# Attention with routing: one last group of nine tiles, and VectorE's extra operations behind a tile's normalisation

## The chip, the cores and the metric

The kernel runs on one core of a Trainium2 chip. Its metric is the device time in microseconds of one execution; the median of three runs of the kernel before is 1285.98 us (1285.92 to 1286.72). The engines are named as the profile names them: PE is TensorE's matmuls and PEld its weight loads, DVE is VectorE, ACT is ScalarE, POOL is GpSimd, and SP issues most of the DMAs.

## The reference, cut to what matters

Three layers follow each other, with 8 batches of 576 tokens, so 4608 tokens of 512 numbers.

```python
# 1: attention, K and V averaged over 8 neighbours first (q, k, v: 8 x 8 heads x 576 x 64)
k_p = k.reshape(B, H, Sp, 8, D).mean(axis=3)
v_p = v.reshape(B, H, Sp, 8, D).mean(axis=3)
s = scale * q @ k_p^T;  s -= max(s);  a = exp(s);  a /= sum(a) + 1e-9
x = a @ v_p                                   # -> 4608 x 512
# 2: mixture of 8 experts
do = x @ w_skip > 0                           # tokens that are computed at all
e = argmax(x @ w_gate);  p = softmax(x @ w_gate)[e]
out = x;  out[do] = x + p * (relu(x @ w1[e]) @ w2[e])      # 512 -> 1024 -> 512
# 3: a dense layer
h = out @ w_in;  g = h * sigmoid(h);  y = g @ w_out        # 512 -> 2048 -> 512
```

## The kernel before, in words

Every operation of an engine is issued through a helper on line 115, so nearly all rows of the profile carry L115 and are told apart by the names of what they write and read. The helper keeps the order in which the code issues them: what stands first in the program for an engine runs first on it.

**Stage 1, attention** (until about 152 us). The 4608 tokens are 36 tiles of 128. Turn i of the loop issues, on PE, the scores `s` of tile i+3, the transposes `pt` of the exponentials of tile i+1, and `pv`, the product with V, of tile i. `pv` has a single PSUM buffer, so that `pv` of tile i+1 waits until DVE has read `pv` of tile i. On DVE the turn issues `mx` (the maxima of tile i+3's scores), some extra operations, and then `post` of tile i: `sm` (sum plus 1e-9), its reciprocal, `cc` (eight router scores and the skip score, per head), `x` (the normalised output, the last reader of `pv`) and `lg` (the router scores of the tile). ACT computes the exponentials `prb` and copies `pts`.

The extra operations are of these kinds. `kp` averages a part of K for a later batch (`pool_k`; the table `KEYS` says in which turns, and six turns have two). `w1l` prepares expert weights in three of the last turns and once more behind. `self.slow` hands out two small operations a turn (`SLOW = 2`). And there is the routing of a group of tiles, in `todo`: when a group's last `lg` is done, `step1` (8 operations, `rmx` to `sb`) finds the expert of each token and writes the one-hot `rohb`, in the next turn `count` lets PE count the tokens of each expert (`rps`, one matmul by `trib` and one by `onesb` for each tile of the group), and `step2` (9 operations, `tot` to `ix`) turns the counts into a place for each token. The numbers A1, A2 and A3 say how many operations of `step1`, of `step2` and of two other small sequences (`choose`, `early`) stand ahead of `post` in their turn; the rest of them stand behind it. For each tile of the group an indirect DMA on POOL then scatters the 128 token numbers to their places in `slots` in DRAM: one or two a turn in the loop, and all of those that are left at the end.

The tiles were grouped as 9, 9, 9, 6 and 3: the fourth group ends with tile 32, and its routing runs in the turns of tiles 33 and 34. The last group of three is routed at the handover.

**Handover** (about 152 to 190 us). The first unit of the experts' layer has its expert chosen and its tokens gathered early (`xn`). PE runs its first layer (`hp`, eight parts f), with `hl` and `hh` made by DVE and ACT. In between, the last group is routed: `step1`, `mm1(0, 1)`, `count`, `step2`, all its scatters. `read_table` on POOL then reads all of `slots` back as `table`, when the scatters have landed. `units` is a long row of tiny DVE operations that plans the other units. DVE's order behind that is: `hl` of part 6, a copy of two thirds of `xr` (`keep`, whose last third is on ACT), `w2l` of parts 0 to 3 (the low halves of the second layer's weights), the rest of `units`, `taken` (`sc` and `table`, which read what `read_table` has brought), the row numbers `gi`, `hl` of part 7, `w2l` of parts 4 to 7. PE's second layer `yp` needs `w2l` part by part. POOL gathers the next unit's tokens by `gi`.

**Stages 2 and 3.** A hardware loop (L1023) runs the other units, and from about 510 us on the dense layer keeps PE busy to the end.

Of the kernel before, what the change touches and what calls it, by code (L numbers as in the profile page):

```python
# [37 lines left out]
U = 3  # L38
# [4 lines left out]
KEYS = {2: (2, 3, 4, 4), 3: (6, 6, 7, 8), 4: (11, 12, 13, 13), 5: (15, 15, 16, 17), 6: (20, 20, 21, 22),  # L43
        7: (24, 24, 25, 26)}
# [8 lines left out]
OPS = [2, 2, 2, 0, 4, 4]  # L53
ORDER = list(range(NT // 512))[::-1]
SLOW = 2
A1, A2, A3 = 8, 5, 12

C_E, C_MV, C_LID, C_WT, C_THR, C_LE, C_UN, C_PK, C_TRI = 0, 2, 13, 49, 57, 153, 217, 241, 265
C_N = C_TRI + P
# [29 lines left out]


GROUP = {}
for _g, (_t0, _n) in enumerate([(0, 9), (9, 9), (18, 9), (27, 6), (33, 3)]):
    GROUP.update({_t0 + _j: (_g, _j, _n) for _j in range(_n)})


# [62 lines left out]
class Kern:  # L158
# [19 lines left out]
    def attention(self, xa, rs, extra):  # L178
        nc, tc, c = self.nc, self.tc, self.c
        self.todo = todo = []  # L180
        self.slow = iter(())
        with tc.tile_pool(name="as", bufs=1) as s1, \
# [31 lines left out]
            def pool_k(b, eng, halves=(0, 2), n=2):  # L214
                k = k_t[b]
                kp = st.get((b, "k"))
                if kp is None:
                    kp = st[b, "k"] = s2.tile([P, 4, G], F32, name=f"kp_{b}", tag="kp")
                if eng is nc.vector:
                    for a in halves:  # L220
                        eng.tensor_reduce(kp[:, a:a + n], k[:, a:a + n], AX.X, ALU.add)
                else:
                    eng.tensor_tensor(k[:, :, :, 0:4], k[:, :, :, 0:4], k[:, :, :, 4:8], ALU.add)
                    eng.tensor_tensor(k[:, :, :, 0:2], k[:, :, :, 0:2], k[:, :, :, 2:4], ALU.add)
                    eng.tensor_tensor(kp, k[:, :, :, 0], k[:, :, :, 1], ALU.add)
# [98 lines left out]
            def pv(t, pt):  # L324
                ps = pp.tile([P, 1024], F32, name=f"pv_{t}", tag="pv")
                ps = ps[:, 0:H * HW].rearrange("p (h e) -> p h e", e=HW)
                for i, j, h0, n, start, stop in PVS:
                    for b, o, r, m in parts(t):
                        ve = vex[b % NB]
                        nc.tensor.matmul(ps[r:r + m, h0:h0 + n, 0:VW], pt[:CP, i, r:r + m], ve[:CP, j:j + n],  # L330
                                         start=start, stop=stop, skip_group_check=True)
                st["pv"] = ps
# [56 lines left out]
            for i in range(-2, NTILE):  # L389
                if i == -2:  # L390
                    pool_v(0, ON0)
                n = 3 if i > DEEP else 2
                if i > 0 and i + n < NTILE:
                    pss = products(i + n)
                    pts[i + 1] = ptrans(i + 1, prs.pop(i + 1))
                    prs[i + n] = scores(i + n, pss)
                elif i != -1 and i <= DEEP:
                    prs[i + 2] = scores(i + 2)
                if len(self.to_place) > (3 if i < EARLY else 0) and i < NTILE - 1:
                    self.place(1, nc.scalar.last)  # L400
                extra(i, True)
                ready = todo.pop(0) if todo and i < NTILE - 1 else None
                if ready and ready[0]:
                    ready[0]()
                if i == -2:
                    values(0)
                    loadv(1)
                    loadq(1)
                if i == -1:
                    pss = products(1)  # L410
                    router1(0)
                if i == 0:
                    pv(0, pts.pop(0))
                if 0 <= i + 1 < NTILE and i + 1 not in pts:
                    pts[i + 1] = ptrans(i + 1, prs.pop(i + 1))
                if i == -1:
                    prs[1] = scores(1, pss)
                    router2(0)
                    pool_k(1, nc.vector, (0,))
                    pool_v(1, ON1)  # L420
                    values(1)
                if i > 0:
                    pv(i, pts.pop(i))
                a = ready[1]() if ready and ready[1] else iter(())
                b = post(i) if i >= 0 else iter(())
                for _ in range(ready[2] if ready else 0):
                    next(a, None)
                for _ in range(SLOW):
                    next(self.slow, None)
                for bb, tiles in KEYS.items():  # L430
                    for r, t in enumerate(tiles):
                        if i == t:
                            pool_k(bb, nc.vector, (r,), 1)
                for _ in b:
                    pass
                for _ in a:
                    pass
                for bb, tiles in KEYS.items():
                    if i == tiles[-1]:
                        keys(bb)  # L440
                if i == 0:
                    pool_k(1, nc.vector, (2,))
                    keys(1)
                for b in range(B):
                    if i + 4 == first[b] and 0 < b < B - 1:
                        loadq(b + 1)
                    if 0 <= i + 2 - first[b] < 2 and 0 < b < B - 1:
                        pool_v(b + 1, 0, ((0,), (1, 2))[i + 2 - first[b]])
                    if i + 2 == first[b]:
                        if b + 2 < B:  # L450
                            loadk(b + 2)
                            loadv(b + 2)
                    if i + 2 == first[b] + 3 + (b == 0) and b + 1 < B:
                        router1(b + 1)
                    if i + 2 == first[b] + 3 and 0 < b < B - 1:
                        values(b + 1)
                    if i + 2 == first[b] + 5 and b + 1 < B:
                        router2(b + 1)
                if i == DEEP:
                    prs[i + 3] = scores(i + 3)  # L460
                if i == EARLY + 7:
                    self.read_table(nc.sync)
                if i == 2:
                    nc.sync.dma_start(self.cb, self.con[:, P + C_TRI:])
                if i == 6:
                    self.consts()
                if i < NTILE - 1:
                    self.place(1, nc.vector.last)
                else:
                    self.place(len(self.to_place))  # L470
                extra(i)
# [373 lines left out]
    def moe(self, xa, up):  # L845
        nc, tc, c = self.nc, self.tc, self.c
        with tc.tile_pool(name="ms", bufs=1) as s1, \
             tc.tile_pool(name="mw", bufs=2) as s2, \
             tc.tile_pool(name="mp", bufs=2, space=PSUM) as pp:
            raw2, xn, xth, xtl, gi, si = self.raw2, self.xn, self.xth, self.xtl, self.gi, self.si  # L850
# [3 lines left out]
            xr = s1.tile([P, U, XW], F32, name="xr", tag="xr")  # L854
            y = self.x4[:, 0:U]

            def keep():
                nc.scalar.copy(xr[:, U - 1], xn[:, U - 1])
                nc.vector.tensor_copy(xr[:, 0:U - 1], xn[:, 0:U - 1])
# [89 lines left out]
            def low2(f):  # L949
                nc.vector.tensor_tensor(self.w2l[:, f], raw2[:, f], self.w2h[:, f].bitcast(F32), ALU.subtract)  # L950

            keep()
            for f in range(4):
                low2(f)
            while not next(units):
# [698 lines left out]
```

## Time and profile before

| | before |
|---|---|
| median of 3 runs | 1285.98 us |
| profiled execution | 1285.66 us |
| its span, first to last instruction | 1283.9 us |
| mean granted TensorE clock | 0.997 |
| PE busy | 1244.5 us, 97% of the span |
| DVE busy | 850.9 us, 66% |
| ACT busy | 576.4 us, 45% |
| POOL busy | 354.8 us, 28% |

The times in the rows are microseconds from the start of the span. A row of the timeline is one instruction or several alike: start, duration, engine, what it writes and reads, shape, count. In square brackets stands how long the engine was idle just before it, and what released it. A row of the windows gives, for each engine, the busy time in a stretch and how many instructions it holds, and then the granted clock of TensorE (1.00 is 2.4 GHz, 0.50 is 1.2 GHz), the mean busy share of the DMA engines and GB/s.

### The profile page before, as it was taken

What the parts mean: (1) busy time and instruction counts of PE and PEld (TensorE: products, weight loads), DVE (VectorE), ACT (ScalarE), POOL (GpSimd) and SP (SyncE); (2) the same over time, 40 slices, a digit from 0 to 9 for tenths busy, and PEclk for the clock granted to TensorE, in tenths of its full rate; (3) what the DMA queues carried; (4) which work ended last, traced back from release to release, by engine and by line L of the source; (5) the groups of instructions that cost most, each with busy time, mean ns of one, the idle gap of its engine ahead of it and who ended that gap; (6) DMA issues with size and microseconds to landing.
All of it is one profiled execution on the core that took longest, in us unless ns stands there. A gap on an engine that the chain in (4) does not pass through costs nothing.

```text
span 1283.9 us, 20146 instructions
## 1 busy us (share of the span) xinstructions
PE 1244.5 (97%) x6469; PEld 1058.2 (82%) x6470; DVE 850.9 (66%) x1559; ACT 576.4 (45%) x1224; POOL 354.8 (28%) x313
## 2 busy tenths in 40 slices
PE   6999899999999989999999999999999999999998
PEld 6988778998888978778888887888888888888887
DVE  5888876666776777889624245656775567846565
ACT  5877534455545554444433344433444233433321
POOL 5477432222222312223377312010201011110100
PEclk9999999999999999999999999999999999999999
DMA  9888536565765634349564225462555444462532
GB/s 372 316 299 287 194 105 236 176 202 173 241 220 187 198 113 144 140 159 305 201 246 145 85 91 174 146 213 93 178 183 186 163 141 139 148 225 94 181 118 88
DMA packets 94716, 234.45 MB, mean 183 GB/s; under 512 B 15093, under 2 KB 27509, under 8 KB 90928
## 3 DMA queue, kind: packets, MB, share of 16 engines
q1 hardware_dynamic: 87344, 216.47, 48.7%
q0 software_dynamic: 7008, 16.80, 4.0%
q8 instruction: 43, 0.70, 0.2%
q14 instruction: 33, 0.27, 0.1%
q10 hardware_dynamic: 288, 0.20, 0.0%
HBM read 183.24 MB, written 52.89 MB: 184 GB/s over the span
## 4 chain that ended last, share of the span: by engine, by line
PE 58%; DVE 2%; issue 1%; ACT 1%; POOL 0%; DMA 0%; ACTq 0%; DVEq 0%; POOLq 0%
PE yb L115 21%; PE ps L115 17%; PE fop L115 8%; PE fh L115 8%; PE hp L115 1%; PE yp L115 1%; DVE fr L115 1%; DVE ft L115 1%; PE fxp L115 1%; DVE fsg L115 0%; PE sx L115 0%; ACT fm L115 0%; DVE fgl L115 0%; ACT g L115 0%; DMA out<-fo 0%
## 5 line engine op out<-in xcount | busy, mean ns | idle before, releaser
L115 PE MATMUL yb<-wout,g 128*128 128x512 f32 x1152 | 268.5, 391 | 0.7 <-DMA wout<-wdo 0.5
L115 PEld LDWEIGHTS yb<-wout,g 128*128 128x128 f32 x1152 | 215.0, 188 | 45.6 <-DMA wout<-wdo 0.9
L115 POOL TENSOR_TENSOR tm<-tm,tm 128x512 f32<-128x512 f32 x24 | 32.2, 1340 | 411.7 <-ACT tm L115 411.7
L115 DVE TENSOR_TENSOR yacc<-yb,yacc 128x512 f32<-128x512 f32 x168 | 116.0, 691 | 38.7 <-PE yb L115 31.4
L115 ACT COPY tm<-ps 128x512 f32<-128x512 f32 x72 | 42.3, 588 | 146.4 <-PE ps L115 144.5
L115 ACT CAST g<-sg 128x512 fp32r<-128x512 f32 x96 | 59.6, 621 | 76.8 <-DVE sg L115 76.8
L115 DVE TENSOR_TENSOR fsg<-fh,fsg 128x512 f32<-128x512 f32 x48 | 33.0, 688 | 83.3 <-ACT fsg L115 80.8
L115 DVE TENSOR_TENSOR w2l<-raw,w2h 128x512 fp32r<-128x512 f32 x96 | 65.8, 690 | 29.0 <-ACT w2h L115 25.5
L115 ACT ACTIVATE hh<-hp 128x256 fp32r<-128x256 f32 (+1 forms) x96 | 39.4, 410 | 98.9 <-PE hp L115 89.2
L115 PE MATMUL fh<-w1l,fh 128*128 128x512 f32 x336 | 83.4, 390 | 0.0
L115 PE MATMUL yp<-w2h,hh 128*128 128x512 f32 x208 | 83.1, 400 | 0.0
L115 PE MATMUL yp<-w2l,hh 128*128 128x512 f32 x208 | 81.2, 391 | 1.9 <-DVE w2l L115 1.9
L115 DVE TENSOR_TENSOR tm<-ps,tm 128x512 f32<-128x512 f32 x24 | 16.6, 691 | 98.1 <-PE ps L115 98.1
L115 PE MATMUL yp<-w2h,hl 128*128 128x512 f32 x208 | 81.3, 391 | 0.0
L115 PE MATMUL hp<-xth,w1h 128*128 128x256 f32 (+2 forms) x384 | 72.5, 311 | 6.6 <-PEq L1650 3.3
L115 PE MATMUL hp<-xtl,w1h 128*128 128x256 f32 (+2 forms) x384 | 72.0, 308 | 3.1 <-DVE xtl L115 1.9
L115 PEld LDWEIGHTS fh<-w1l,fh 128*128 128x128 f32 x336 | 62.8, 188 | 12.9
L115 PE MATMUL hp<-xth,w1l 128*128 128x256 f32 (+2 forms) x384 | 71.2, 308 | 0.0
L115 ACT ACTIVATE prb<-s,mx 128x72 f32<-128x72 f32 x288 | 65.3, 355 | 11.0 <-DVE mx L115 11.0
L115 DVE TENSOR_TENSOR g<-sg,g 128x512 fp32r<-128x512 f32 x96 | 65.8, 686 | 5.1 <-ACT g L115 4.8
L115 PEld LDWEIGHTS hp<-xth,w1h 128*128 128x128 f32 x384 | 60.4, 192 | 9.4 <-issue 7.6
L115 PE MATMUL fop<-fh,fgh 128*128 128x512 f32 x168 | 66.4, 395 | 1.2 <-ACT fgh L115 1.2
(240 smaller groups left out, 2723.1 us busy)
## 6 DMA issues: line engine op xcount, KB each, us to landing
raw<-w SPq DMA_DIRECT2D x88, 512.0 KB, 4.4
wout<-wdo SPq DMA_DIRECT2D x48, 512.0 KB
win<-wdi SPq DMA_DIRECT2D x36, 512.0 KB
w1l<-wdi SPq DMA_DIRECT2D x36, 512.0 KB
xa<-x SPq DMA_DIRECT2D x36, 256.0 KB
fx<-xa SPq DMA_DIRECT2D x9, 1024.0 KB
v<-vR SPq DMA_DIRECT2D x7, 1280.0 KB
fr<-w_in SPq DMA_DIRECT2D x16, 512.0 KB
```

Of the source, the lines that this page charges most:

```text
L115: ins = f(*a, **k)
```

## The change: what it does

There are five edits. The numbers A1, A2, A3 become 5, 0, 5. The last two groups become one group of nine. `count` is issued behind `pv` of its turn. Of the extra operations only the first part of `kp` and the first A operations of the routing stand ahead of `post`; the second `kp`, the rest of the routing and then the two slow operations stand behind it. At the handover the copy to `xr` is three ACT copies instead of one on ACT and one on DVE.

```diff
-A1, A2, A3 = 8, 5, 12
+A1, A2, A3 = 5, 0, 5
...
-for _g, (_t0, _n) in enumerate([(0, 9), (9, 9), (18, 9), (27, 6), (33, 3)]):
+for _g, (_t0, _n) in enumerate([(0, 9), (9, 9), (18, 9), (27, 9)]):
...
                 ready = todo.pop(0) if todo and i < NTILE - 1 else None
-                if ready and ready[0]:
-                    ready[0]()
...
                 if i > 0:
                     pv(i, pts.pop(i))
+                if ready and ready[0]:
+                    ready[0]()
                 a = ready[1]() if ready and ready[1] else iter(())
                 b = post(i) if i >= 0 else iter(())
                 for _ in range(ready[2] if ready else 0):
                     next(a, None)
+                todays = [(bb, r) for bb, tiles in KEYS.items() for r, t in enumerate(tiles) if i == t]
+                for bb, r in todays[:1]:
+                    pool_k(bb, nc.vector, (r,), 1)
+                for _ in b:
+                    pass
+                for bb, r in todays[1:]:
+                    pool_k(bb, nc.vector, (r,), 1)
+                for _ in a:
+                    pass
                 for _ in range(SLOW):
                     next(self.slow, None)
-                for bb, tiles in KEYS.items():
-                    for r, t in enumerate(tiles):
-                        if i == t:
-                            pool_k(bb, nc.vector, (r,), 1)
-                for _ in b:
-                    pass
-                for _ in a:
-                    pass
...
-            keep()
+            for j in range(U):
+                nc.scalar.copy(xr[:, j], xn[:, j])
             for f in range(4):
                 low2(f)
```

On DVE, in the turn of tile 10, which has the second step of the first group's routing, the kernel before runs five operations of that step (`tot` to `pi`) ahead of the tile's `sm`:

```order
L115 TENSOR_REDUCE mx_790<-s_774 128x4
L115 TENSOR_REDUCE mx_790<-s_777 128x4
L115 TENSOR_TENSOR tot_76<-tot_75,rps_801 128x8
L115 TENSOR_TENSOR ra_819<-rps_801,tot_75 128x72
L115 TENSOR_TENSOR ra_819<-ra_819,rohb_759 128x72
L115 TENSOR_REDUCE ri_822<-ra_819 128x9
L115 TENSOR_SCALAR pi_824<-ri_822 128x9
L115 TENSOR_SCALAR sm_826<-pv_812 128x8
L115 RECIPROCAL sm_826<-sm_826 128x8
L115 TENSOR_TENSOR cc_827<-pv_812,sm_826 128x72
L115 TENSOR_TENSOR x_84<-pv_812,sm_826 128x512
L115 TENSOR_REDUCE lg_769<-cc_827 128x9
```

In the changed kernel the same place reads:

```order
L115 TENSOR_REDUCE mx_790<-s_774 128x4
L115 TENSOR_REDUCE mx_790<-s_777 128x4
L115 TENSOR_SCALAR sm_818<-pv_801 128x8
L115 RECIPROCAL sm_818<-sm_818 128x8
L115 TENSOR_TENSOR cc_819<-pv_801,sm_818 128x72
L115 TENSOR_TENSOR x_84<-pv_801,sm_818 128x512
L115 TENSOR_REDUCE lg_763<-cc_819 128x9
L115 TENSOR_TENSOR tot_76<-tot_75,rps_807 128x8
L115 TENSOR_TENSOR ra_827<-rps_807,tot_75 128x72
L115 TENSOR_TENSOR ra_827<-ra_827,rohb_768 128x72
L115 TENSOR_REDUCE ri_830<-ra_827 128x9
L115 TENSOR_SCALAR pi_832<-ri_830 128x9
```

The five operations have moved from ahead of `sm` to behind `lg`, where the other four of the step follow them, as before.

On PE, in the same turn, the kernel before runs the count (`rps`, by `trib` and then nine times by `onesb`) between the transposes and `pv`:

```order
L115 MATMUL pt_781<-ident,prb_117 120x128 x3
L115 MATMUL pt_786<-ident,prb_117 120x128 x2
L115 LDWEIGHTS trib
L115 MATMUL rps_801<-rohb_759,trib 128x72
L115 LDWEIGHTS onesb
L115 MATMUL rps_801<-rohb_759,onesb 128x72
```

In the changed kernel `pv` stands there first:

```order
L115 MATMUL pt_781<-ident,prb_117 120x128 x3
L115 MATMUL pt_786<-ident,prb_117 120x128 x2
L115 MATMUL pv_801<-vex_114,pts_721 128x2x74
L115 MATMUL pv_801<-vex_114,pts_721 128x3x74
L115 MATMUL pv_801<-vex_114,pts_721 128x2x74 x3
L115 LDWEIGHTS trib
L115 MATMUL rps_807<-rohb_768,trib 128x72
```

The count has moved behind `pv`, as in the two other groups that are counted in the loop.

On POOL, from the end of the loop to the first gather of the handover, the difference is this (`pad_w` is a small memset that follows the loop):

```order
 L115 DMA slots<-consts,ix_1967 36864x1 x9
-L115 DMA slots<-consts,ix_2235 36864x1 x6
-L115 MEMSET pad_w_2310 128x1
-L115 DMA slots<-consts,ix_2409 36864x1 x3
+L115 MEMSET pad_w_2252 128x1
+L115 DMA slots<-consts,ix_2357 36864x1 x9
 L115 DMA table<-slots 128x288
```

The scatters are as many as before, but all nine of the last group now stand behind the memset, one row of nine directly ahead of the read of the table.

## Rows read from the trace of the kernel before

**Rows 1.** The page, first section: busy time, share of the span and instructions.
```profile
PE 1244.5 (97%) x6469; PEld 1058.2 (82%) x6470; DVE 850.9 (66%) x1559; ACT 576.4 (45%) x1224; POOL 354.8 (28%) x313
```

**Rows 2.** Waits of PE, 20 to 150 us: total, times, longest.
```profile
PE pv L115 <- DVE x L115: 7.0, 8, 1.8
```

**Rows 3.** Timeline of PE: the waits of pv for x in the loop, and one count.
```profile
55.29 0.38 PE L115 MATMUL rps<-rohb,onesb 128*128 128x72 bf16 x9
55.92 1.63 PE L115 MATMUL pv<-vex,pts 120*128 120x148 f32 x10 [0.24 <-DVE x L115]
76.94 1.63 PE L115 MATMUL pv<-vex,pts 120*128 120x148 f32 x10 [0.93 <-DVE x L115]
88.38 1.63 PE L115 MATMUL pv<-vex,pts 120*128 120x148 f32 x10 [0.73 <-DVE x L115]
95.43 1.63 PE L115 MATMUL pv<-vex,pts 120*128 120x148 f32 x10 [0.67 <-DVE x L115]
110.98 1.63 PE L115 MATMUL pv<-vex,pts 120*128 120x148 f32 x10 [0.76 <-DVE x L115]
```

**Rows 4.** Timeline of DVE, tiles 10, 15 and 20.
```profile
56.60 0.15 DVE L115 TENSOR_TENSOR tot<-tot,rps 128x8 f32<-128x8 f32 x1
...
57.58 0.17 DVE L115 TENSOR_SCALAR sm<-pv 128x8 f32<-128x8 f32 x1
...
60.92 0.16 DVE L115 TENSOR_SCALAR sm<-pv 128x8 f32<-128x8 f32 x1
...
75.52 0.17 DVE L115 TENSOR_SCALAR sm<-pv 128x8 f32<-128x8 f32 x1 [0.73 <-PE s L115]
...
92.71 1.40 DVE L115 TENSOR_REDUCE kp<-k 128x72 f32<-128x576 f32 x2
```

**Rows 5.** Timeline of DVE, the last turns of the loop.
```profile
145.78 0.17 DVE L115 TENSOR_SCALAR sm<-pv 128x8 f32<-128x8 f32 x1 [1.46 <-PE xtp L115]
...
147.15 0.16 DVE L115 TENSOR_SCALAR pf<-pi 128x6 f32<-128x6 int32 x1
...
147.83 1.02 DVE L115 TENSOR_TENSOR xtl<-xtp,xth 128x384 fp32r<-128x384 f32 x2
...
149.89 0.15 DVE L115 SCALAR_TENSOR_TENSOR start<-sc,pick 1x8 f32<-1x8 f32 x1
...
150.17 0.15 DVE L115 TENSOR_SCALAR sm<-pv 128x8 f32<-128x8 f32 x1
```

**Rows 6.** Timeline of POOL at the handover.
```profile
159.92 0.98 POOL L115 DMA_INDIRECT slots<-consts,ix  x1 [3.84 <-DVE ix L115]
...
162.49 0.98 POOL L115 DMA_INDIRECT slots<-consts,ix  x1 [0.30 <-issue]
165.66 0.60 POOL L115 DMA_DIRECT2D table<-slots  x1 [2.19 <-DMA slots<-consts,ix]
```

**Rows 7.** Windows at the handover, where no other DMA runs.
```profile
167.40:168.00 0.60, 0.60 (x6) 0.60 (x5) 0.56 (x3) 0.56 (x2) 0.00 (x0) 1.00 0.24 92
168.00:168.60 0.60, 0.60 (x4) 0.34 (x2) 0.60 (x2) 0.08 (x1) 0.00 (x0) 1.00 0.00 0
```

**Rows 8.** Timeline of DVE at the handover.
```profile
168.07 0.68 DVE L115 COPY xr<-xn 128x1040 f32<-128x1040 f32 x1
171.44 0.17 DVE L115 TENSOR_TENSOR sc<-table,m 128x24 f32<-128x24 f32 x1
```

**Rows 9.** Timeline of PE at the handover.
```profile
169.41 0.50 PE L115 MATMUL yp<-w2l,hh 128*128 128x512 f32 x1 [0.69 <-DVE w2l L115]
173.66 0.50 PE L115 MATMUL yp<-w2l,hh 128*128 128x512 f32 x1 [1.22 <-DVE w2l L115]
```

**Rows 10.** Windows in the units' loop, around a gap of PE.
```profile
355.90:359.30 3.40, 1.41 (x10) 1.07 (x9) 3.18 (x5) 0.00 (x0) 0.31 (x1) 1.00 0.90 293
359.30:362.80 3.50, 3.50 (x19) 3.50 (x18) 2.12 (x5) 0.90 (x3) 1.51 (x1) 0.51 0.74 274
362.80:366.20 3.40, 3.40 (x31) 3.40 (x31) 2.24 (x4) 1.97 (x5) 2.04 (x2) 1.00 0.64 172
```

## The prediction

> **What bounds the kernel now.** I read the page's busy shares first: PE is busy for 1244.5 us, 97% of the span, and no other engine for more than two thirds [rows 1]. So time can be won or lost only where PE idles, or where it gets more to do. The change touches the attention's 36 tiles and the handover to the experts' units, so the second view is PE's waits there: the largest is `pv` waiting for DVE's `x` of the tile before, 8 times, 7.0 us together [rows 2]. The third view, PE's timeline, says where: five of the eight stand in the loop's middle, 0.24, 0.93, 0.73, 0.67 and 0.76 us, 3.33 together [rows 3]; the other three, 3.7 us, are in the last turns. The fourth, DVE's timeline, says what DVE did ahead of the late `x`. The fifth is the handover: POOL's scatters, the read of the table behind them, DVE's use of it, and PE's waits for `w2l`, which DVE makes behind that [rows 6 to 9].
>
> **The loop: extra operations behind `post`.** The edits can give back at most the stalls that extra operations cause. At tile 10 it is 0.24 (step 1 ahead of `post`), at tile 19 0.73 (the same), at tile 21 0.67 and at tile 25 0.76 (two `kp`, 1.40 together, ahead of `sm` [rows 4]). Sum: 2.40. The fifth, 0.93, comes behind a `sm` that itself had waited 0.73 for PE, with the `kp` long done [rows 4]; I count it in the bound only: 2.40 + 0.93 = 3.33.
>
> Against that stand two costs. First, the count: ten matmuls, of which the nine by `onesb` take 0.38 [rows 3]. Ahead of `pv` they lay in PE's time of waiting, where a wait followed (0.24 left behind them, and 0.73); behind `pv` nothing covers them. So of 0.24 + 0.73 up to 2 x 0.38 = 0.76 comes back as work: 0.97 - 0.76 = 0.21 is left. Second, the five operations of step 2: from 56.60 to 57.58 they take 0.98, and the `sm` behind them then starts at 57.58, while `pv` of that tile, started at 55.92, took 1.63 and was over at 57.55 [rows 3, 4]. They filled time in which DVE would have waited for PE. Behind `post` they push the next `mx`, the next `kp` and the next `sm` (60.92 before) by up to 0.98 less what the earlier step leaves free. About half of that I take to arrive in the next `sm`, and the three times that there are (one for each group of nine in the loop) make 3 x 0.5 = 1.5 of DVE lateness. Some of it meets slack, some becomes a wait of `pv`.
>
> So the loop: gains 0.21 + 0.67 + 0.76 = 1.64 against up to 1.5. I take 0.0 for the sum. Bounds: -3.3 (all five stalls go, nothing comes back) and +1.6 (no stall goes, since `mx` and the first `kp` still stand ahead, and 3 x 0.5 arrives).
>
> **The last turns.** The routing of the six-tile group falls away. Its `step1` and the first five operations of `step2` lie ahead of a `sm` that waited 1.46 for PE, so they cost nothing; the last four (147.15 to 147.83, 0.68) stand on DVE's chain, which the first `hp` waits for. That is -0.68. The two slow operations of that turn, which lay under the wait of 1.46, now stand behind `lg`: +0.28, from the pair at 149.89 to 150.17 [rows 5]. That pair itself moves from ahead of one `post` to behind it and stays on the chain. -0.68 + 0.28 = -0.4; I take -0.3, since the last group's `step1` is now nine wide. Bounds: -1.5 (the wait of 1.46 shrinks as well) and +0.3.
>
> **The handover, the largest term.** Nine scatters stand where three stood. POOL issues them one behind the other, at 159.92 and 162.49 the first and the third: (162.49 - 159.92) / 2 = 1.285 each, 0.98 of it busy, 0.30 its own issue [rows 6]. Six more: 6 x 1.285 = 7.71. The last starts at 170.20 instead of 162.49, and the table's read, which waits for all of them to land (2.19 of waiting), is issued at 165.66 + 7.71 = 173.37. Before, its data moved until about 168.0: the share of the DMA engines is 0.24 up to there and nothing behind [rows 7], so it was there 2.3 after the issue, and DVE needed it only at 171.44 [rows 8]. That is a slack of 3.4, which hides 3.4 of 7.71. Now the table is there at 173.37 + 2.3 = 175.7. DVE waits; behind `sc` in its queue stand `table`, `gi`, `hl` of part 7, all four `w2l` of the second half, and for `w2l` PE waits. From `sc` to PE's start on that half it was 173.66 - 171.44 = 2.22 [rows 8, 9], so PE starts it at 175.7 + 2.2 = 177.9: +4.3. PE stands from about 172 on for some 6 us, in place of 1.22 [rows 9]. The next unit's gather waits for `gi` and moves by the same 4.3, so nothing is won behind it. Bounds: +3.7, if the data lay there already at 167.4, and +5.
>
> The third of the count: six more matmuls, 6 x 0.38 / 9 = 0.25 at most, in PE's row of `hp`; 0.1 of it reaches `ix`. The copy to `xr`: 0.68 leaves DVE, so the first `w2l` is early and PE's wait of 0.69 goes; but what PE wins there it loses at the second half, which waits for the table whatever stands ahead of it: 0. ACT's two more copies stand ahead of the `hh` of part 7, which has time until 177.9: 0; without that cover the copy would be worth -0.7.
>
> **The clock.** In the units' loop a stretch in which PE was busy for 1.41 of 3.40 us is followed by one at 0.51, which is 1.2 GHz, with 19 matmuls, and then by one at 1.00, 2.4 GHz, with 31 [rows 10]. A gap of 6 us is longer than the 2 us of that one. At the lower level PE lost (31 - 19) / 31 x 3.4 = 1.3 us. PE is the bound behind the gap (the rest of `yp`, transposes), so I take +1.3; bounds 0 (the fall lies within the gap) and +2.6 (two such stretches). The Trainium skill, "TensorE: Matmul & The Clock Gate", section "HAM oscillation — how this bites in real kernels", says that gaps in which PE waits for data let the clock fall back to half in the middle of a kernel; the row agrees.
>
> **Sum.** 0.0 - 0.3 + 4.3 + 0.1 + 1.3 = +5.4 on the profiled execution's 1285.66, its span of 1283.9 and 1.8 around it: 1291.1. The median of the runs is 0.3 above that execution, which is noise here; I forecast 1291.0.
>
> **Rivals.**
> - *Not slower: the loop pays for the late table.* The four stalls and some of the last turns' 3.7 us go, and the late `sm` meets slack. For it: every stall of rows 3 has extra operations of DVE ahead of it, and PE gets no more work than before. Against it: the bounds of the two parts, -3.3 and -1.5, must nearly both be reached to balance 4.3 and the clock. It decides from a gain of 2.9 on, since 5.7 - 2.9 = 2.8 is near what a measurement tells from nothing. At -3.3, without the clock's fall: 1285.7 - 3.3 - 0.7 + 4.4 = 1286.1; with it, 1287.4.
> - *Faster: the scatters overlap.* If POOL's pace were a matter of how far DVE lies behind and not of each scatter, six more would fit into the slack of 3.4, from 3.4 / 6 = 0.57 apiece down. The gain of loop and last turns would then stand alone, with 0.7 of the copy: 1285.7 - 0.3 - 0.7 - 1.6 = 1283.1. Against it: the pitch of 1.285 in rows 6, where nothing but the issue stands between. The Trainium skill, "DMA: Bandwidth & Descriptors", "Anatomy of one DMA — SWDGE (gpsimd) path", calls descriptor generation small and says that many descriptors can be emitted before a cost shows. By that the six would be hidden; the 0.98 of busy time on POOL for each speaks against it.
> - *The clock stays.* Late table as above, no fall: 1291.1 - 1.3 = 1289.8. For it: the gap may end such that the fall lies inside it.
> - *Worse.* The operations behind `post` arrive whole, +1.6, and the clock falls for two stretches, +2.6 in place of 1.3: 1291.1 + 1.6 + 1.3 = 1294.0.
>
> **Chances.** Forecast (1290 to 1292) 0.42; clock stays 0.20; worse 0.13; loop pays 0.19; overlap 0.06. What a measurement of this kernel can tell from no change is about 0.2%, 2.6 us: 1283.4 to 1288.6. Faster: most of the overlap and a little of the loop, 0.07. Same: most of the loop's case and a part of the two others, 0.18. Slower: 0.75. Range: 1286.6 to 1293.2, which leaves out the overlap, the best of the loop's case and the worst of the worse; the forecast's own range is 1289 to 1292.5.
>
> **What would show it.** Nine scatters on POOL at the handover, 1.285 apart, and the table's read issued some 7.7 later than before; a new wait of DVE's `sc` for the table of 4 to 5 us; PE's wait of `yp` for `w2l` of about 6 in place of 1.22; a granted clock of about 0.5 in the stretch behind. In the loop: the waits at tiles 21 and 25 shorter, but new waits of `pv` two tiles behind the second step of a group. I am wrong if the scatters are closer together than 0.6, if PE's waits in the loop fall by more than 3, or if the table's read needs much less than 2.3.

## The result and the profile after

The changed kernel takes 1294.24 us (median, 1293.41 to 1295.55) against 1285.95 us for the kernel before: 1.0066 times, with a 95% interval of 1.0051 to 1.0080. It is slower, as forecast, but by 8.3 us instead of 5, and it lies above the range's upper end of 1293.2. The profiled execution took 1293.42 us, its span 1291.7. The first section of its page, which answers to [rows 1]: PE has 4 us more of busy time, DVE, which lost operations, 2 less.

```profile
PE 1248.7 (97%) x6468; PEld 1061.5 (82%) x6469; DVE 849.2 (66%) x1541; ACT 577.8 (45%) x1226; POOL 355.1 (27%) x313
```

PE's waits in the loop, 20 to 150 us (total, times, longest), answering to [rows 2]:

```profile
PE pv L115 <- DVE x L115: 6.0, 6, 2.2
PE pv L115 <- DVE vex L115: 1.2, 1, 1.2
PE s L115 <- ACT prb L115: 1.2, 2, 0.6
```

The wait of `pv` for `x` fell by 1.0, but a new kind came up: PE's scores `s` wait for ACT's exponentials. PE's timeline, one such wait, the longest wait of `pv` (tile 25, 0.76 before [rows 3]), the end of part 6 of `hp`, and `yp`'s wait, answering to [rows 9]:

```profile
41.67 0.76 PE L115 MATMUL s<-kbd,q 128*128 128x144 f32 x4 [0.62 <-ACT prb L115]
...
112.55 1.63 PE L115 MATMUL pv<-vex,pts 120*128 120x148 f32 x10 [2.22 <-DVE x L115]
...
166.80 0.85 PE L115 MATMUL hp<-xth,w1l 128*128 128x384 f32 x4
...
174.66 0.80 PE L115 MATMUL yp<-w2l,hh 128*128 128x512 f32 x1 [4.69 <-DVE w2l L115]
```

POOL's timeline, the first and the last of the nine scatters and the read of the table, answering to [rows 6]:

```profile
160.05 0.98 POOL L115 DMA_INDIRECT slots<-consts,ix  x1 [7.29 <-DVE ix L115]
...
170.32 0.98 POOL L115 DMA_INDIRECT slots<-consts,ix  x1 [0.30 <-issue]
172.98 0.60 POOL L115 DMA_DIRECT2D table<-slots  x1 [1.68 <-DMA slots<-consts,ix]
```

That is the row of nine that was foretold: (170.32 - 160.05) / 8 = 1.284 each, and the read at 172.98 (173.37 in the prediction). But it is not what DVE waited for. DVE's timeline, which answers to [rows 8], and ACT's, the `hh` of parts 5 and 6:

```profile
173.45 0.56 DVE L115 SCALAR_TENSOR_TENSOR hl<-hp,hh 128x384 fp32r<-128x384 f32 x1 [3.89 <-ACT hh L115]
...
176.68 0.17 DVE L115 TENSOR_TENSOR sc<-table,m 128x24 f32<-128x24 f32 x1
```

```profile
167.20 0.49 ACT L115 ACTIVATE hh<-hp 128x384 fp32r<-128x384 f32 x1 [2.67 <-remote]
...
172.93 0.49 ACT L115 ACTIVATE hh<-hp 128x384 fp32r<-128x384 f32 x1 [4.73 <-remote]
```

`sc` did not wait at all. DVE had waited 3.89 for `hh` of part 6, which ACT started at 172.93, though the matmuls of part 6 end at 166.80 + 0.85 = 167.65: as the trace reads, PE's result reached ACT 5.3 us late, at the moment at which POOL's last scatter had landed (172.98). The profile names only `remote` as what released ACT, so that it was PE's result that came late is a reading of these times. PE then waited 4.69 for the first `w2l`, not for the second half. The windows show the clock, the level of 1.2 GHz behind that gap, and once more in the units' loop:

```profile
170.90:174.30 3.40, 0.00 (x0) 0.00 (x0) 0.85 (x2) 1.37 (x3) 1.00 (x2) 0.69 0.04 6
174.30:177.70 3.40, 3.04 (x7) 2.46 (x8) 2.81 (x10) 2.10 (x5) 0.00 (x0) 0.50 0.12 38
177.70:181.10 3.40, 3.40 (x13) 2.70 (x13) 3.33 (x10) 0.00 (x0) 2.13 (x2) 0.81 0.18 35
...
223.40:226.80 3.40, 3.29 (x10) 3.32 (x11) 1.62 (x3) 0.00 (x0) 0.98 (x1) 0.50 0.08 22
```

So two questions: what the loop lost, and whether the late table or PE's late results make the handover's cost.

### The profile page after: what moved, and what is told of

The parts are those of the page before. It is cut to its first block, busy times and chain, and to the rows that moved or that the text cites. A ratio compares the mean times of both kernels' runs of the same rounds, so it can differ in the third digit from the quotient of the medians.

```text
span 1291.7 us, 20123 instructions
## 1 busy us (share of the span) xinstructions
PE 1248.7 (97%) x6468; PEld 1061.5 (82%) x6469; DVE 849.2 (66%) x1541; ACT 577.8 (45%) x1226; POOL 355.1 (27%) x313
## 4 chain that ended last, share of the span: by engine, by line
PE 58%; DVE 3%; issue 1%; ACT 1%; POOL 0%; DMA 0%; DVEq 0%; ACTq 0%; POOLq 0%
PE yb L115 21%; PE ps L115 17%; PE fh L115 9%; PE fop L115 9%; PE yp L115 1%; DVE fr L115 1%; DVE ft L115 1%; PE fxp L115 1%; DVE raw L115 0%; PE sx L115 0%; DVE fgl L115 0%; DVE fsg L115 0%; DVE w2l L115 0%; PE hp L115 0%; ACT g L115 0%
## 5 line engine op out<-in xcount | busy, mean ns | idle before, releaser
L115 ACT ACTIVATE fsg<-fh 128x512 f32<-128x512 f32 x48 | 28.7, 599 | 90.2 <-PE fh L115 86.9
```

The costliest lines, as they stand in the source:

```text
L115: ins = f(*a, **k)
```

## The experiments

**How they are read.** The start of the program (to the `pv` of tile 3) differs by up to 3.4 us from one execution to the next, and single runs by several us, so beside the times two stretches are read from each profile. A goes from the `pv` of tile 3 to the `pv` of the last tile (the loop), B from there to the first `hp` of the units' loop (the handover; the row of PE that had waited 0.62 for the loop's branch). Within one kind of execution A of the same loop agrees to 0.2 us. There are two kinds: in one, PE's results reach DVE and ACT late wherever scatters are under way, as above and as in [rows 4] and [rows 5], where `sm` waits for PE; in the other they do not. The six late profiles are the first pair, whose chip is not on record, and those of one chip (e1 to e4); the other twelve come from two other chips. No known chip shows both kinds, so the kind may belong to the chip and not to the execution. The medians of the kernel before point to the chip (1288.72 us on that of e1 to e4, 1285.22 and 1285.40 on the two others), but the first pair's 1285.95 does not.

Behind B the profiles differ too, by up to 7.5 us (1093.63 from there to the end in e1, 1101.08 in e5), and also between kernels that are alike there (1095.52 in f1, 1099.95 in g1). That is nearly as much as the whole effect, and it stands in neither A nor B. A and B tell where an edit loses time; only the medians tell how much a kernel loses in all.

| kernel | A | B | against the kernel before of the same kind |
|---|---|---|---|
| *results late* | | | |
| kernel before | 116.93 | 42.41 | |
| changed kernel | 118.22 | 46.45 | +1.29, +4.04 |
| e1_group_only | 115.71 | 47.65 | -1.22, +5.24 |
| e2_order_only | 118.82 | 42.81 | +1.89, +0.40 |
| e3_six_more | 116.80 | 49.33 | -0.13, +6.92 |
| e4_three_of_nine | 119.95 | 41.25 | +3.02 (a stretch at the lower clock in it), -1.16 |
| *results on time* | | | |
| f1_before_again | 113.50 | 42.06 | |
| f2_after_again | 115.78 | 49.00 | +2.28, +6.94 |
| f3_group_again | 113.54 | 49.24 | +0.04, +7.18 |
| f4_keep_act | 113.56 | 41.45 | +0.06, -0.61 |
| e5_table_first | 115.78 | 41.23 | +2.28, -0.83 |
| e6_second_kp | 113.95 | 43.63 | +0.45, +1.57 |
| e7_count_behind | 118.43 | 42.14 | +4.93, +0.08 |
| e8_steps_behind | 119.95 | 44.63 | +6.45, +2.57 |
| g1_best | 112.79 | 41.45 | -0.71, -0.61 |
| g2_seven | 115.78 | 42.13 | +2.28, +0.07 |
| g3_order_again | 115.77 | 44.33 | +2.27, +2.27 |
| g4_three_again | 115.76 | 41.28 | +2.26, -0.78 |

**e1: the group alone.** The kernel before with

```diff
-... [(0, 9), (9, 9), (18, 9), (27, 6), (33, 3)]
+... [(0, 9), (9, 9), (18, 9), (27, 9)]
```

> The kernel before with the groups 9, 9, 9, 9 alone; nothing else is changed. Theory, the row of scatters: nine scatters at the handover, 1.285 us apart, hold back what PE has finished (ACT's hh of parts 5 and 6 start 2 to 5 us after the end of their hp) and bring the table some 7.7 us later, so 1290 to 1293 us, with a wait of yp for w2l of 3 to 5 us and a stretch at the lower clock behind it; the first hp up to 0.7 us earlier than at 152.1. Rival, the order in the loop: the time comes from the operations behind post and the later count, so this kernel is at 1285 to 1287 us.

1.0022 times (1.0009 to 1.0036). B is 5.24 longer, and A 1.22 shorter, since the last turns have less to do. The handover's loss belongs to the group, but the time, 2.8 us, is less than half of the whole.

**e2: the order alone**, the changed kernel with that line put back.

> The changed kernel with the groups 9, 9, 9, 6, 3 put back; the order in the loop, the later count and the three ACT copies stay. Theory, the row of scatters: the handover is as before, yp waits for w2l under 1.5 us twice, no lower clock there; what is left is the loop, the first hp 0.5 to 1.5 us later than 152.1, so 1286 to 1288 us. Rival, the order in the loop: 1291 to 1294 us.

1.0043 times (1.0027 to 1.0058), 5.5 us: more than the theory allows, and A is 1.89 longer (another 2.5 of its profile stand behind B). The rival was right that the order costs something of its own, which the prediction had at nothing.

**e3: six scatters more.** The kernel before, whose last group issues its three scatters twice into spare arrays first:

```diff
-            def slot(j, t):
+            def slot(j, t, to=None):
...
-                    self.slots, ...
+                    self.slots if to is None else to, ...
...
+            if g == 4:
+                self.to_place += [lambda j=j, to=to: slot(j, t0 + j, to) for to in self.spare for j in range(n)]
```

> The kernel before with six more scatters at the handover, ahead of the last group's three, of the same row numbers into two spare arrays that nothing reads; nothing else is changed. Theory, the row of scatters: as with the groups of nine, 1290 to 1292 us, ACT's hh of parts 5 and 6 late by 2 to 5 us. Rival, the wider last group itself (its step on DVE, six more matmuls of the count): no change, 1285 to 1287 us.

1.0053 times (1.0032 to 1.0074). No wider group, and B grows by 6.92; the scatters are the cost. ACT's `hh` of part 6 and PE's wait:

```profile
171.80 0.49 ACT L115 ACTIVATE hh<-hp 128x384 fp32r<-128x384 f32 x1 [4.80 <-remote]
```

```profile
174.15 0.80 PE L115 MATMUL yp<-w2l,hh 128*128 128x512 f32 x1 [6.53 <-DVE w2l L115]
```

**e4: six scatters fewer**, the changed kernel with

```diff
+            self.to_place = self.to_place[6:]
             self.place(len(self.to_place))
```

> The changed kernel without the first six of the last group's nine scatters, so the tokens of six tiles get no place and keep the value of the attention; the units and their sizes are planned from the same counts. Theory, the row of scatters: 1286 to 1288.5 us, ACT's hh of parts 5 and 6 within 1 us of the end of their hp, yp's wait for w2l under 1.5 us. Rival, the wider group or the order in the loop: 1292 to 1295 us as the changed kernel.

1.0017 times (1.0002 to 1.0032): 2.2 us are left of 8.3 (0.3 to 4.1), as the theory said, and B is shorter than before.

**e5: the table first**, the changed kernel with the read of the table moved ahead of the scatters:

```diff
+            self.read_table(nc.gpsimd)
             self.place(len(self.to_place))
...
-            self.read_table(nc.gpsimd)
```

> The changed kernel with the read of the table issued ahead of the last group's nine scatters, so that the tokens of the last nine tiles are missing from the table and get no place; the scatters themselves, the plan and the units' sizes stay. It tells the late table from the late results of PE. If the table holds up the first unit, as the prediction has it, the first long wait of yp for w2l (4.7 us in the changed kernel) falls under 1.5 us. If the results of PE, which reach ACT late while the row of scatters runs, hold it up, hh of part 6 still starts 3 to 6 us behind the end of its hp and yp still waits 3 to 7 us, the table being there long before.

One run, 1289.18 us beside 1286.48. PE's results were on time here, all nine scatters were issued, and B is 0.83 shorter than before (yp's wait for `w2l` is 1.20). Where results are on time, then, nine scatters cost the handover nothing by themselves; what costs is that the table waits for them. The time is no lower for it, since A is 2.28 longer and the stretch behind B is the longest of all. This did not settle the other kind, since late results did not occur.

**e6, e7, e8: the order in pieces.** The kernel before with one piece each: the second `kp` behind `post`; `ready[0]()` behind `pv`; and `A1, A2, A3 = 5, 0, 5`.

> The kernel before with the second kp of a turn behind post, and nothing else. Measured from the pv of tile 3 to the first hp, the kernel before takes 121.86 us, and with all edits of the order (groups 9, 9, 9, 6, 3) it took 2.75 more. If the later maxima, by way of ACT's exponentials, hold up PE's scores, this edit brings the waits of s at tile 6 (+0.7) and tile 15 (+0.9) and takes the waits of pv at tiles 16 (-0.9), 21 and 25 (-0.7 each): +0 to +1 in all. If the second kp is harmless, -1.5 to -2.5, with no new wait of s.

> The kernel before with the count of the experts behind pv, and nothing else. If it is ten matmuls' time that is moved from under a wait into the open: from the pv of tile 3 to the first hp 0 to +0.8 us on 121.86, in steps of up to 0.4 at tiles 11, 20 and 30, with nothing gained at tiles 10 and 19 beyond their waits of 0.24 and 0.73. If DVE's step 2, which now waits for the later count ahead of sm, holds up x: +1.5 to +3.

> The kernel before with the numbers 5, 0, 5 (three operations of step 1 and all of step 2 behind post), and nothing else. If operations behind post delay the next maxima and with them ACT's exponentials and PE's scores: new waits of s at tiles 11 and 30, of pv for vex at tile 31, from the pv of tile 3 to the first hp +0.5 to +2 us on 121.86. If they only lift the stalls of tiles 10 and 19: -0.5 to -1.

One run each: 1291.80, 1291.38 and 1290.46 us beside 1286.48. PE's waits in the loop, e6 first, then e7, then e8:

```profile
PE pv L115 <- DVE x L115: 4.0, 6, 1.1
PE s L115 <- ACT prb L115: 1.2, 2, 0.6
```

```profile
PE pv L115 <- DVE x L115: 9.0, 11, 1.9
```

```profile
PE rps L115 <- DVE rohb L115: 4.7, 4, 1.9
```

In e6 the waits of `pv` shrink (4.9 in f1, below) and two waits of `s` take their place: +0.45 in A, inside the first theory's 0 to 1. In e7 the second theory had the right cause and too small a price: with the count behind `pv` and half of step 2 still ahead of `sm`, DVE's `tot` waits for the count (`rps`, 5.3 us in four waits), and A grows by 4.93. In e8 neither theory had the main cause: with `rohb` behind `post` and the count still ahead of `pv`, PE itself waits for `rohb`, 4.7 us, and A grows by 6.45. A part of e8's A, and of B in e6 and e8, is a stretch at 1.2 GHz (146.0 to 149.4 us in e8, 152.3 to 155.7 in e6). So these two pieces belong together; each alone is worse than both.

**f1 to f4: the pair again, the group and the copy, beside each other.** f1 is the kernel before, f2 the changed one, f3 repeats e1, and f4 is the kernel before with

```diff
-            keep()
+            for j in range(U):
+                nc.scalar.copy(xr[:, j], xn[:, j])
```

> The kernel before, unchanged, for a profile beside the next three. In the runs so far PE's results reached DVE and ACT late, by 0.3 to 5 us, wherever scatters were under way, in six profiles, and hardly at all in four taken later. If that belongs to the scatters of the program, this profile shows the waits of pv at tiles 16 and 25 (0.9 and 0.8 us) again and the first hp 121.9 us behind the pv of tile 3; if it comes and goes with the execution, they are gone in some and the first hp comes 2.5 to 4 us sooner.

> The changed kernel, unchanged, beside the kernel before of the same call. If late results of PE make the handover's wait, and they are absent here, yp's first wait (4.7 us) is gone, and the late table, which the prediction names, shows: DVE's sc waits 3 to 5 us for it and yp waits 4 to 6 us at the second half of w2l; 5 to 9 us slower than before. If they are there, as the first profile of this kernel.

> The kernel before with groups of nine alone. With late results of PE: yp waits 4 to 6 us once, at the first w2l. Without: DVE's sc waits for the table, yp waits once at the second half, 4 to 6 us, and the time is 2 to 5 us over the kernel before in both.

> The kernel before with the three copies to xr on ACT, and nothing else. If the copy on DVE stands ahead of the w2l that yp waits for first: the first wait of yp (0.69) is gone, the second stays at 1.2, the units' loop is entered 0.5 to 0.9 us sooner behind the first hp. If the second wait takes the gain: no change.

f1 1.0007 (0.9993 to 1.0022), f2 1.0053 (1.0030 to 1.0075), f3 1.0058 (1.0039 to 1.0077), f4 0.9996 (0.9978 to 1.0014). In all four PE's results were on time. f1's A is 3.4 shorter than in the first profile of the same kernel, so the late results are no property of the program; and the changed kernel still loses, in another way. By the times the group alone (f3) costs as much as the whole change (f2), though in the profiles f2 has 2.24 more in A: the two losses do not add up in the medians, and five runs each do not tell why. Waits of PE, 20 to 147 us, f1 and then f2:

```profile
PE pv L115 <- DVE x L115: 4.9, 7, 1.1
PE pv L115 <- DVE vex L115: 0.5, 1, 0.5
```

```profile
PE pv L115 <- DVE x L115: 3.7, 5, 1.0
PE s L115 <- ACT prb L115: 1.8, 3, 0.6
PE pv L115 <- DVE vex L115: 1.2, 1, 1.2
...
PE s L115 <- ACT vt L115: 0.4, 1, 0.4
```

`pv` waits 1.2 less, `s` 2.2 more and `vex` 0.7 more: +1.7 of the loop's 2.3. The rest is no wait of PE; PE is busy for 0.73 longer in A (108.50 against 107.77), which fits a count that now lies in the open, but no run has that alone. From the starts of `pv` in PE's timelines it can be read where the loop loses; the stretches that are left out differ by 0.04 at most:

| from the `pv` of tile | f1 | f2 | f2 - f1 | e6 - f1 | what was moved there |
|---|---|---|---|---|---|
| 5 to 7 | 6.42 | 7.13 | +0.71 | +0.71 | second `kp` |
| 9 to 12 | 9.99 | 10.49 | +0.50 | 0.00 | step 1, count, step 2 |
| 14 to 16 | 6.41 | 7.13 | +0.72 | +0.73 | second `kp` |
| 18 to 21 | 11.55 | 11.04 | -0.51 | -0.93 | both |
| 24 to 25 | 3.20 | 3.05 | -0.15 | -0.12 | second `kp` |
| 28 to 31 | 11.81 | 12.94 | +1.13 | +0.02 | step 1, count, step 2 |
| 31 to 35 | 12.75 | 12.61 | -0.14 | 0.00 | routing of the six-tile group, gone |

So the second `kp` alone makes 0.45 of the 2.28 (e6). The other 1.83 come with the routing: the difference of f2 and e6, not a run of its own. PE's timeline, f1 and then f2 (the `pv` of tile 3, in f2 two waits of `s`, the last `pv`, the second half of `yp`):

```profile
29.32 1.55 PE L115 MATMUL pv<-vex,pts 120*128 120x148 f32 x10
...
142.82 1.61 PE L115 MATMUL pv<-vex,pts 120*64 120x148 f32 x20 [0.80 <-DVE x L115]
...
168.94 0.50 PE L115 MATMUL yp<-w2l,hh 128*128 128x512 f32 x1 [1.23 <-DVE w2l L115]
```

```profile
29.35 1.55 PE L115 MATMUL pv<-vex,pts 120*128 120x148 f32 x10
...
40.61 0.76 PE L115 MATMUL s<-kbd,q 128*128 128x144 f32 x4 [0.62 <-ACT prb L115]
...
125.97 0.76 PE L115 MATMUL s<-kbd,q 128*128 128x144 f32 x4 [0.55 <-ACT prb L115]
...
145.13 1.61 PE L115 MATMUL pv<-vex,pts 120*64 120x148 f32 x20 [0.80 <-DVE x L115]
...
176.34 0.79 PE L115 MATMUL yp<-w2l,hh 128*128 128x512 f32 x1 [7.08 <-DVE w2l L115]
```

The wait of 0.62 at 40.61 shows how `s` comes to wait. DVE's and ACT's timelines of f2 ahead of it:

```profile
37.33 0.74 DVE L115 TENSOR_REDUCE kp<-k 128x72 f32<-128x576 f32 x1
```

```profile
38.11 0.96 ACT L115 ACTIVATE kbd<-kp,consts 128x288 f32<-128x288 f32 x2 [0.74 <-DVE kp L115]
38.98 0.73 ACT L115 COPY pts<-pt 120x384 f32<-120x384 f32 x2
39.60 0.54 ACT L115 ACTIVATE prb<-s,mx 128x72 f32<-128x72 f32 x2
```

In this turn the second `kp` is the last part of its batch, and ACT makes `kbd` from it. ACT stands in order: it waits 0.74 for the `kp` that now lies behind `post`, the copies and the exponentials behind `kbd` start late, and PE cannot write new scores until they have been read.

The wait of 0.55 at 125.97, in the turn with the third group's count, has the routing ahead of it. DVE's and ACT's timelines of f2:

```profile
123.13 1.14 DVE L115 TENSOR_TENSOR rohb<-roh,rdo 128x72 bf16<-128x72 f32 x1
...
124.48 0.81 DVE L115 TENSOR_REDUCE mx<-s 128x4 f32<-128x288 f32 x2
```

```profile
124.96 1.80 ACT L115 ACTIVATE prb<-s,mx 128x72 f32<-128x72 f32 x8 [1.29 <-DVE mx L115]
```

The last three operations of step 1 stand behind `post` now, and so ahead of the next `mx`; `prb` waits for `mx` and `s` for `prb`. Besides, these three took 1.99 here, while POOL was busy with a gather and with `vex` (122.25 to 125.25), and 0.62 in f1, where POOL stood idle beside them.

POOL and DVE at the handover of f2:

```profile
156.57 0.98 POOL L115 DMA_INDIRECT slots<-consts,ix  x1 [7.31 <-DVE ix L115]
...
165.56 3.27 POOL L115 DMA_INDIRECT slots<-consts,ix  x1 [0.30 <-issue]
169.14 0.98 POOL L115 DMA_INDIRECT slots<-consts,ix  x1 [0.30 <-issue]
171.79 0.60 POOL L115 DMA_DIRECT2D table<-slots  x1 [1.68 <-DMA slots<-consts,ix]
```

```profile
174.28 0.18 DVE L115 TENSOR_TENSOR table<-table,sc 128x24 f32<-128x24 f32 x1 [5.87 <-DMA table<-slots]
```

Here is the predicted wait: DVE stands 5.87 for the table, which comes 174.28 - 171.79 = 2.5 behind its issue, and PE 7.08 for the second half of `w2l`. (It is the operation behind `sc` that waits; `sc` itself runs at 168.25.) One thing more was not foreseen: the eighth scatter took 3.27 in place of 0.98. DVE's first half of `w2l` had started just ahead of it:

```profile
165.50 2.48 DVE L115 TENSOR_TENSOR w2l<-raw,w2h 128x512 fp32r<-128x512 f32 x4
```

The scatter ends at 165.56 + 3.27 = 168.83, 0.85 after DVE's row (167.98). All 18 profiles agree on this (last section): what matters is what DVE does beside a scatter, and not that it is the eighth. The clock behind PE's wait:

```profile
174.10:177.50 3.40, 1.16 (x3) 0.97 (x4) 2.63 (x7) 0.00 (x0) 1.11 (x1) 0.50 0.00 0
177.50:180.90 3.40, 3.40 (x10) 2.63 (x9) 2.62 (x14) 0.53 (x2) 2.47 (x2) 0.50 0.60 157
```

f4 gives 0.61 in B, in the profile alone; the time tells no change.

**g1 to g4: what was still open.** g1 is f4 with the second `kp` behind `post` where no `kbd` waits for it:

```diff
+                ahead = 1 if i in (15, 20, 24) else 2
+                for bb, r in todays[:ahead]:
...
+                for bb, r in todays[ahead:]:
```

g2 is the changed kernel with `self.to_place = self.to_place[2:]` ahead of the last scatters; g3 and g4 repeat e2 and e4.

> The kernel before with the two edits that gave something by themselves: the three copies to xr on ACT, and the second kp behind post, but only in the turns of tiles 15, 20 and 24, where no scores of PE wait behind it. From the pv of tile 3 to the first hp 0.5 to 1.2 us less than the kernel before of the same kind of execution, 0.4 to 0.9 less at the handover: 0.05 to 0.15% faster, which may be less than can be measured.

> The changed kernel without the first two of the last group's nine scatters, so the tokens of two tiles get no place; the plan and the units' sizes stay. In three profiles the eighth scatter of the row took 3.3 to 3.9 us instead of 0.98. If that belongs to its place in the row (or to the count of scatters since the start less two), no scatter of the seven takes over 1.4, and DVE's wait for the table falls from 5.9 to about 1 us (2 x 1.285 for the two, 2.3 for the stall). If a scatter stalls at a certain time whatever its number, the sixth takes 3.3 and DVE's wait is about 3.3.

> The changed kernel with the groups 9, 9, 9, 6, 3. Where PE's results are not late, from the pv of tile 3 to the first hp it takes 2.3 us more than the kernel before (118.44 there), as the changed kernel did, 0.6 come back at the handover by the copy, and the end is 1.5 to 3 us later: 0.1 to 0.25%. If the loss of the loop needs the group of nine, no more than 0.5.

> The changed kernel without the first six of the last group's nine scatters (the tokens of six tiles get no place). Where PE's results are not late: DVE does not wait for the table, yp waits 1.2 us, no lower clock behind the handover, and what is left is the loop's loss: 1 to 3 us over the kernel before. If the wider step and count of the group cost by themselves, 4 or more.

g1 1.0000 (0.9986 to 1.0014): its profile is 1.3 shorter over A and B, but that cannot be told in the time, so no version was found that measurably beats the kernel before. g2 1.0028 (1.0013 to 1.0042): no scatter stalls, DVE waits 0.82 for the table and PE 2.05:

```profile
169.07 0.18 DVE L115 TENSOR_TENSOR table<-table,sc 128x24 f32<-128x24 f32 x1 [0.82 <-DMA table<-slots]
```

```profile
171.12 0.50 PE L115 MATMUL yp<-w2l,hh 128*128 128x512 f32 x1 [2.05 <-DVE w2l L115]
```

The 5 us between 5.87 and 0.82 are the two scatters (2.6) and the stall (2.3). The expectation asked whether the stall goes with the place in the row or with a certain time. It goes with neither: the seventh scatter was over at 165.08, and `w2l` started at 165.33, so that no scatter met it. g3 1.0040 (1.0024 to 1.0055): A has the same +2.27 as the changed kernel, so the loop's loss needs no group of nine; with the six-tile group still there, B is 2.27 longer, which the expectation of a gain there missed: step 2 of that group now stands behind `post` and ahead of `xtl`, the first `hp` waits 1.79 for `xtl` (1.11 in f1), and a stretch at a granted clock of 0.59 follows. g4 1.0027 (1.0011 to 1.0042): B is 0.78 shorter than before, and A and B together are 1.48 longer, which is the loop's loss less this; the time's 3.5 us (1.4 to 5.4) holds more, and that stands behind B.

## Why the prediction was too low

**Right: the side and the handover's mechanism, where PE's results are on time.** From the last `pv` to the second half of `yp` f1 takes 168.94 - 142.82 = 26.12, f2 176.34 - 145.13 = 31.21: +5.1, where 4.3 + 0.1 stood. The pitch of 1.285 and the 2.3 to 2.5 of the table hold. That the sum comes so near is in part luck. The table's read of f1:

```profile
161.47 0.60 POOL L115 DMA_DIRECT2D table<-slots  x1 [3.46 <-DMA slots<-consts,ix]
```

It is issued 161.47 - 142.82 = 18.65 behind the last `pv`, and 171.79 - 145.13 = 26.66 behind it in f2: 8.0 more, near the 7.71 of the sum. But the scatter beside `w2l`, which the prediction did not look at, added 2.3, and the shorter wait for the landing (1.68 in place of 3.46) took 1.8 away. Of the 8.0, 2.9 were hidden, where 3.4 stood.

**Right in kind, too small: the clock.** 1.3 was forecast, with 2.6 as the upper bound. From the second half of `yp` to the units' loop f2 takes 1.85 more than f1, with two stretches at 0.50.

**Wrong: the loop.** This is the step that failed: "gains 0.21 + 0.67 + 0.76 = 1.64 against up to 1.5. I take 0.0 for the sum", with +1.6 as the upper bound. On time it is +2.28 in every kernel with the whole order. In the table above, three stretches gain 0.80 together and four lose 3.06, so the step was wrong on both sides. The gains: the stalls of 0.93 and 0.76 in [rows 3] are not there in f1, where PE's results are on time, so extra operations alone do not make them. The first had been put into the bound alone; the second was counted as a gain, and moving the second `kp` of that turn gives 0.12 (e6). The costs: operations behind `post` were priced at 3 x 0.5, by the next `sm` and so by `pv`, and the second `kp` behind `post` at nothing. It was ACT that passed the lateness on: `kbd` waits in ACT's queue for the moved `kp` (+0.71 and +0.72, at tiles 6 and 15), `prb` waits for an `mx` that the routing has pushed back (+1.13, tiles 28 to 31, with `pv` waiting for `vex` there as well), and PE's `s` waits for `prb`. The prediction did not ask who else waits for the operations that were moved.

**The last turns**, forecast at -0.3: on time the loop's last stretch gives -0.14 (table), and PE's first `hp` waits 0.76 for `xtl` in f2 and 1.11 in f1, which is in the 5.1 above. Where results are late, the group gives -1.22 with the old order (e1).

**The sum.** On time: 2.3 + 5.1 + 1.85, less 0.45 that comes back later, is the 8.8 between the spans of f2 and f1 (1289.2 and 1280.4). In the first pair of profiles, with late results: 1.29 in the loop and 0.15 ahead of it, 4.04 at the handover, and 2.3 behind it, of which the stretch at 223.40 has more than half: PE had waited there 2.61 where the kernel before waited 2.24, and behind that one the clock stayed at 1.00. Together 7.8, the difference of the spans (1291.7 and 1283.9). Against the forecast this pair has 1.7 more up to the last `pv`, 1.7 less at the handover with its clock (4.04 for 5.7), and 2.3 more behind it, where nothing had been forecast. The length of PE's wait does not decide whether the clock falls: in f1, the kernel before again, the wait at that place was 2.23, and the lower clock followed. The kernel before and then f1, behind that wait:

```profile
217.30:220.70 3.40, 3.39 (x18) 3.24 (x19) 0.41 (x2) 0.74 (x2) 0.97 (x1) 1.00 0.27 103
```

```profile
212.20:215.60 3.40, 3.36 (x11) 3.39 (x12) 0.37 (x2) 0.00 (x0) 0.97 (x1) 0.51 0.22 80
```

That this lower clock falls in one execution and not in the next was in the range, but not where it came.

**The rivals.** The loop did not pay: it lost. The scatters do not overlap: their pitch is the old one. The clock did not stay. "Worse" came nearest (1294.0): the loop's loss and two stretches at the lower clock are both in the trace, but the loss came by way of ACT and the second stretch in the units' loop, so the nearness is in part luck.

**What stays open.** Why PE's results reach the other engines late beside scatters in some profiles, and whether that goes with the chip. (That a scatter of the row of nine stalls only in the other kind is no riddle: in the changed kernel's first profile DVE, held up by `hh`, started `w2l` at 173.93, behind the last scatter.) For the measured pair itself the late results are what the trace shows at the handover (ACT at 172.93); that the table, issued at 172.98, would have held DVE up there if they had not, is argued from f2 and not shown in that execution.

## What to carry to other kernels

When an operation is moved behind others, list all who wait for it, on every engine's queue, and not only the next reader that the edit has in mind: the second `kp` held up ACT, and ACT the scores. Two edits that hand a value to each other (here the one-hot, its count and the step behind it) are to be moved together and priced together. Joining small groups at a point that everything waits for moves all of their slow DMAs to that point: with results on time nine scatters there made B 7 us longer, seven 0.1, and three nothing. And ask what other engines do beside such a row: DVE's `w2l` added 2.3 to it.

## What the runs showed of the hardware that was not expected

- Beside scatters of 128 single numbers, ACT and DVE started on PE's results up to 5.3 us after the recorded end of the matmul, in the six profiles of one kind and hardly in the twelve of the other. The loop of the same kernel is 3.4 us longer for it (116.93 against 113.50).
- A scatter that starts while DVE makes `w1l` or `w2l` (subtractions of two arrays), or in f3 the copy to `xr` directly ahead of `w2l`, ends 0.85 or 0.86 us after DVE's row. That holds for all 13 such scatters in the 18 profiles, which took 1.35 to 3.89 in place of 0.98: in f1 `w1l` ends at 145.61 and the scatter at 146.47, and the 3.28 of e5 and the 3.89 of f3 are the same stall. Scatters that started ahead of DVE's row took 0.98 to 1.02, and the gathers of `xn` beside the second half of `w2l` were held up little (1.11 and 1.47 in f2). Why is not shown.
- The same gap of PE can set off a stretch at 1.2 GHz in one execution and not in another: behind 2.24 us the granted clock was 1.00, and behind 2.23 at the same place of the same kernel 0.51.
